# First batch's values in 1 KB pieces, key sums by one-column products, and the split of a times b one step earlier

## The chip, the cores and the metric

One core of a Trainium2 chip runs the whole kernel. The metric is the device time in microseconds (us). Matrix products run on TensorE (PE, with its weight loads PEld), elementwise work on VectorE (DVE) and ScalarE (ACT), some fills and a few tensor operations on GpSimd (POOL), and transfers are issued by SyncE (SP).

## The reference, cut to what matters

Linear attention, a gated pair of products, and a mixture of four experts, all in float32:

```python
q_s = exp(q - max(q, -1));  q_s /= sum(q_s, -1) + 1e-9
k_s = exp(k - max(k, 2));   k_s /= sum(k_s, 2) + 1e-9      # over the 576 tokens
kv  = einsum('bhsd,bhse->bhde', k_s, v)
x   = einsum('bhsd,bhde->bhse', q_s, kv)                    # then (2304, 512)
a, b = x @ w1, x @ w2                                       # 512 -> 1024
h = (a * b) @ w3;  x = h @ w_out                            # back to 512
out = sum_e p[:, e] * (relu(x @ w1[e]) @ w2[e])             # 4 experts
```

q, k and v have 4 batches, 8 heads, 576 tokens and 64 values per head. The weights of the gated pair arrive as 64-bit floats and are turned into float32 on the chip.

## The kernel before, in words

The work is written as one Python program, and a scheduler then lays down, for each engine, the order in which its instructions run; each engine takes its own list strictly in order and waits on semaphores. SP's list is one queue of transfers that has eight completion semaphores in rotation, so that a transfer also waits for the one eight places ahead of it.

Heads are taken in pairs, in the order `PAIRS`. For a pair of batch `b`, `load_k` and `load_v` (lines 185 to 205) fetch keys and values: 128 partitions hold four tokens each (512 tokens), and 64 partitions hold a tail of one token each (`KX`, the last 64). The tile of values has 65 columns per token; column 65 is filled with ones by POOL (line 197). A token's 64 values are therefore followed by a gap in the tile, and line 200 writes them in pieces of 256 bytes, while the tail is fetched by line 203. `k_max` finds the keys' largest values (DVE lines 225 to 236, PE lines 232 and 238, ACT line 244), `k_exp` subtracts and exponentiates (lines 254 and 257), and `k_v` (line 269) multiplies five times per pair: the exponentiated keys are the weights of the product, the 130 columns of values and ones stream past. The column of ones so gives the keys' sums, whose reciprocals `rs` (lines 276 and 279) scale the copy into `bd` (line 283).

Queries go through `q_exp` and `q_norm` (lines 292, 307, 311, 324 to 327) in two halves per batch, are transposed by PE (line 339), copied by ACT (line 341), multiplied by `bd` (line 352, tile `xp`), and split into a high and a low part (lines 368, 369, 373). `ab_step(c, f)` (lines 110 to 112 from line 499 on) multiplies a chunk of 512 tokens by slice `f` of both weights and stores a times b in `ah`. Each product is done in three: high by high, high by low, low by high.

The weights need a conversion (`convert`): a transfer `f64` (line 436), ACT line 141, DVE lines 145, 148, 152 and 156, and a split into `wg` (ACT line 104, DVE line 105). `unit` multiplies w3 by w_out into `W`. `h_step` splits `ah` into the two parts `h` (lines 104 and 105), which `y_step` multiplies by `W`. In the loop over `steps` (16 steps, two chunks of eight slices) the split runs four steps ahead of the product. The experts fill the rest of the run, from some 350 us on.

The first batch's part of `k_v` and the first slices of `ab_step` are what the change touches at the start of the run; the loop over `steps` is around 200 to 300 us.

Of the kernel before, what the change touches and what calls it, by code (L numbers as in the profile page):

```python
# [33 lines left out]


PAIRS = [0, 2, 1, 3]
FILL_T, FILL_B, FILL_V = (5, 3, 3, 12), (0, 3, 3, 0), (0, 0, 0, 0)
K_SLOT = [[0, 0, 0, 0], [6, 7, 8, 9], [30, 32, 34, 36], [46, 47, 48, 50]]
Q_SLOT = [[2, 2], [6, 8], [30, 34], [46, 48]]
# [17 lines left out]
def linear_attention_moe_kernel(ctx: ExitStack, tc, q, k, v, w1, w2, w3, wo, dp, e1, e2, out):  # L57
# [35 lines left out]
    def bank(pool, name):  # L93
        return pool.tile([P, 512], F32, tag="b", name=name)
# [17 lines left out]
        return nc.tensor.matmul(out=ps, lhsT=w_lo, rhs=r_hi, start=False, stop=last, **kw)  # L112

    ones = const.tile([P, 256], BF16, name="ones")
    busy = {}

    def keep_busy(n, i=None):
# [66 lines left out]
    def load_k(b, hp):  # L184
# [7 lines left out]
        ))  # L192
        kraw[b, hp] = t

    def load_v(b, hp):
        t = ap_.tile([P, 2, KR + 1, D + 1], F32, tag="vt", name="vt", bufs=4)
        nc.gpsimd.memset(t[..., D:D + 1], 1.0)
        src = v[b, 2 * hp:2 * hp + 2]
        for h in range(2):
            hold("pace" if b > 2 else ("in", b), nc.sync.dma_start(  # L200
                out=t[:, h, 0:KR, 0:D], in_=src[h, 0:KR * P].rearrange("(p r) d -> p r d", p=P)
            ))
        hold("pace" if b > 2 else ("in", b), nc.sync.dma_start(
            out=t[0:KX, :, KR, 0:D], in_=src[:, KR * P:S].rearrange("h p d -> p h d")
        ))
        vt[b, hp] = t
# [55 lines left out]
    def k_v(b, hp):  # L262
        ek, vv = ekt.pop((b, hp)), vt.pop((b, hp))
        bd = ap_.tile([P, P], F32, tag="bd", name="bd", bufs=2)
        nc.gpsimd.memset(bd, 0.0)
        ps = bank(ps_w if b == 0 else ps_a, "kv")
        for r in range(KR + 1):
            p = P if r < KR else KX
            i = nc.tensor.matmul(  # L269
                out=ps[:, 0:2 * D + 2], lhsT=ek[0:p, r].rearrange("p h d -> p (h d)"),  # L270
                rhs=vv[0:p, :, r, :], start=r == 0, stop=r == KR,
            )
        if b == 0:
            keep_busy(FILL_V[PAIRS.index(hp)], i)
        rs = ap_.tile([P, 1], F32, tag="rs", name="rs", bufs=2)
        nc.vector.tensor_scalar(
            out=rs, in0=ps[:, D:D + 1], scalar1=1e-9, scalar2=None, op0=ALU.add
        )
        nc.vector.reciprocal(out=rs, in_=rs)
        for h in range(2):  # L280
            p = slice(D * h, D * h + D)
            o = (D + 1) * h
            nc.scalar.activation(  # L283
                out=bd[p, D * h:D * h + D], in_=ps[p, o:o + D], func=ACTF.Copy, scale=rs[p]
            )
        kvb[b, hp] = bd
# [224 lines left out]
    def h_step(c, f):  # L511
        n = chunks[c][1]
        h = gran("h")
        split(h[:, 0, 0:n], h[:, 1, 0:n], prods[c, f // 2][:, f % 2, 0:n])
        if f % 2:
            del prods[c, f // 2]
        hg[c, f] = h
# [219 lines left out]

    keep_busy(14)
    make_identity(nc, ident)
    nc.scalar.activation(out=nident, in_=ident, func=ACTF.Copy, scale=-1.0)  # L740
    for i in range(4):
        load_k(0, PAIRS[i])
# [31 lines left out]
    for f in range(NF):  # L774
        convert(17 + f // 2)
        slot(W1 + f, (unit, 8 + f))
        if f % 2:
            h_step(*steps[f // 2])
    finish_lo(*prev.pop(0))
    wog.clear()  # L780
    conv.close()
# [9 lines left out]
    for i, (c, f) in enumerate(steps):  # L791
        if c == 1 and f >= NF - 2:
            load_w12(2, f - NF + 2)
        if i + 4 < len(steps):
            h_step(*steps[i + 4])
        slot(Y0 + i, (y_step, c, f))
        if i > 2:
            cook_some(2)
        if f == NF - 1:
            y_out(c)  # L800
# [298 lines left out]
```

## Time and profile before

| | us |
|---|---|
| median of 3 runs | 1159.44 |
| lowest, highest | 1158.41, 1159.78 |
| profiled execution, its own time | 1159.13 |
| span of the profiled execution | 1157.3 |
| PE busy | 1129.5 (98%) |
| DVE busy | 868.3 (75%) |
| ACT busy | 535.4 (46%) |
| POOL busy | 43.5 (4%) |

The span is what the trace covers; the profiled execution's own time lies 1.83 us above it. PE is busy nearly throughout, and where it isn't lies in the first tenth of the run. A matmul's end is modelled, so a busy PE can still be a PE that could go faster. Instructions on PE come as pairs, a weight load and the product; a float32 product without a split takes two such pairs, so that five products of line 269 are ten records.

### The profile page before, as it was taken

How to read it: one execution, taken by the hardware profiler on the slowest of the kernel's cores; microseconds unless marked ns; L12 is line 12 of the kernel's file. 1: busy time of each engine (PE TensorE's matmuls, PEld its weight loads, DVE VectorE, ACT ScalarE, POOL GpSimd, SP SyncE). 2: the span in 40 equal slices, each digit the busy share in tenths (PEclk: the TensorE clock that was granted, in tenths of full speed). 3: DMA queues.
4: the chain of work that ended last, by engine and by line, in shares of the span. 5: the costliest groups of instructions: out<-in, count | busy, mean ns of one | idle time of the engine just before them, and what ended most of it. 6: DMA issues, size and time to landing. Idle time of an engine off the chain costs nothing.

```text
span 1157.3 us, 18802 instructions
## 1 busy us (share of the span) xinstructions
PE 1129.5 (98%) x7091; PEld 1049.2 (91%) x7091; DVE 868.3 (75%) x1429; ACT 535.4 (46%) x982; POOL 43.5 (4%) x70
## 2 busy tenths in 40 slices
PE   7798999999999999999999999999999999999997
PEld 5566888788888889999999999999999999999997
DVE  7998766685558444999999987777779877777777
ACT  4775445454445325655545544334335344443441
POOL 0012100112010000000000000000000000000000
PEclk9999999999999999999999999999999999999999
DMA  9998850789899976877877888777777797777773
GB/s 236 272 351 301 322 196 1 200 288 404 311 315 369 346 290 232 294 287 281 295 271 287 280 310 304 252 247 252 247 254 258 240 308 252 253 250 251 250 253 110
DMA packets 127418, 310.12 MB, mean 268 GB/s; under 512 B 31968, under 2 KB 52960, under 8 KB 127328
## 3 DMA queue, kind: packets, MB, share of 16 engines
q1 hardware_dynamic: 126848, 308.14, 77.5%
q8 instruction: 56, 0.92, 0.3%
q10 hardware_dynamic: 480, 0.79, 0.2%
q14 instruction: 34, 0.28, 0.1%
HBM read 232.33 MB, written 76.55 MB: 267 GB/s over the span
## 4 chain that ended last, share of the span: by engine, by line
PE 87%; DVE 6%; DMA 4%; SPq 2%; issue 1%; ACT 1%; DVEq 0%; ACTq 0%
PE hp L913 30%; PE op L987 27%; PE ab L110 5%; PE ab L112 5%; PE ab L111 5%; PE y L110 3%; PE y L112 3%; PE y L111 3%; PE W L110 1%; DVE acc L971 1%; PE W L111 1%; PE W L112 1%; DMA qr<-in_q_dram 1%; PE kv L269 1%; PE xp L352 1%; DMA kr<-in_k_dram 1%
## 5 line engine op out<-in xcount | busy, mean ns | idle before, releaser
L987 PE MATMUL op<-eg,h 128*128 128x256 f32 x3024 | 379.9, 280 | 0.1
L913 PE MATMUL hp<-t,eg 128*128 128x384 f32 x2016 | 376.6, 336 | 0.9 <-DVE acc L971 0.9
L987 PEld LDWEIGHTS op<-eg,h 128*128 128x128 f32 x3024 | 373.4, 188 | 0.6 <-DVE acc L971 0.3
L913 PEld LDWEIGHTS hp<-t,eg 128*128 128x128 f32 x2016 | 344.6, 188 | 2.5 <-DVE acc L971 1.9
L971 DVE SCALAR_TENSOR_TENSOR acc<-op,prob,acc 128x256 f32<-128x256 f32 (+1 forms) x396 | 198.0, 530 | 43.1 <-PE op L987 43.1
L104 ACT ACTIVATE h<-blk 128x768 fp32r<-128x768 f32 x168 | 138.0, 843 | 142.7 <-DVE blk L614 108.9
L105 DVE TENSOR_TENSOR h<-blk,h 128x768 fp32r<-128x768 f32 x168 | 157.5, 954 | 24.4 <-ACT h L104 24.3
L896 ACT ACTIVATE blk<-hp 128x384 f32<-128x384 f32 x192 | 90.6, 489 | 142.2 <-PE hp L913 140.4
L900 DVE TENSOR_TENSOR blk<-hp,blk 128x384 f32<-128x384 f32 x144 | 79.6, 558 | 67.7 <-PE hp L913 67.2
L112 PE MATMUL ab<-x,wg 128*128 128x512 f32 (+1 forms) x320 | 119.8, 375 | 2.9 <-DVE wg L105 2.8
L110 PE MATMUL ab<-x,wg 128*128 128x512 f32 (+1 forms) x320 | 120.9, 379 | 0.9 <-ACT bd L283 0.5
L111 PE MATMUL ab<-x,wg 128*128 128x512 f32 (+1 forms) x320 | 118.7, 371 | 0.2 <-ACT x L373 0.2
L902 ACT ACTIVATE blk<-blk 128x768 f32<-128x768 f32 x72 | 60.6, 845 | 72.7 <-DVE blk L900 71.0
L614 DVE TENSOR_TENSOR blk<-blk 128x768 f32<-128x768 f32 x96 | 91.6, 954 | 0.5
L112 PEld LDWEIGHTS ab<-x,wg 128*128 128x128 f32 x320 | 60.3, 188 | 14.7 <-DVE wg L105 4.8
L110 PEld LDWEIGHTS ab<-x,wg 128*128 128x128 f32 x320 | 60.2, 189 | 12.3 <-ACT wg L104 1.4
L111 PEld LDWEIGHTS ab<-x,wg 128*128 128x128 f32 x320 | 60.4, 189 | 10.9 <-ACT x L373 1.2
L105 DVE TENSOR_TENSOR eo<-e2r,eo 128x512 fp32r<-128x512 f32 x56 | 39.1, 708 | 23.9 <-ACT eo L104 23.6
L508 DVE TENSOR_TENSOR ah<-ab,ah 128x512 f32<-128x512 f32 (+1 forms) x40 | 25.4, 635 | 40.9 <-PE ab L112 40.6
L111 PE MATMUL y<-h,W 128*128 128x512 f32 x128 | 50.2, 394 | 0.0
L112 PE MATMUL y<-h,W 128*128 128x512 f32 x128 | 49.9, 395 | 0.0
L110 PE MATMUL y<-h,W 128*128 128x512 f32 x128 | 46.8, 400 | 0.0
(101 smaller groups left out, 1044.3 us busy)
## 6 DMA issues: line engine op xcount, KB each, us to landing
eg<-e_t SPq DMA_DIRECT2D x96, 512.0 KB, 4.6
eg<-e_b SPq DMA_DIRECT2D x72, 512.0 KB, 5.0
eg<-e_s SPq DMA_DIRECT2D x68, 512.0 KB, 4.4
eg<-e_a SPq DMA_DIRECT2D x51, 512.0 KB, 4.6
wg<-w SPq DMA_DIRECT2D x48, 512.0 KB, 8.8
f<-in_moe_w_dram SPq DMA_DIRECT2D x32, 512.0 KB, 6.6
e_t<-eo SPq DMA_DIRECT2D x32, 512.0 KB, 7.5
e_s<-eg SPq DMA_DIRECT2D x28, 512.0 KB, 4.4
```

Source lines behind the costliest of these rows:

```text
L104: i = nc.scalar.activation(out=hi, in_=src, func=ACTF.Copy)
L105: j = eng.tensor_tensor(out=lo, in0=src, in1=hi.bitcast(F32), op=ALU.subtract)
L110: nc.tensor.matmul(out=ps, lhsT=w_hi, rhs=r_hi, start=first, stop=False, **kw)
L111: nc.tensor.matmul(out=ps, lhsT=w_hi, rhs=r_lo, start=False, stop=False, **kw)
L112: return nc.tensor.matmul(out=ps, lhsT=w_lo, rhs=r_hi, start=False, stop=last, **kw)
L614: return lambda: nc.vector.tensor_tensor(out=dst, in0=x, in1=y, op=op)
L896: nc.scalar.activation(out=block(name)[:, u], in_=src, func=func)
L900: nc.vector.tensor_tensor(out=x[:, u], in0=src, in1=x[:, u], op=ALU.add)
L902: nc.scalar.activation(out=x, in_=x, func=ACTF.Relu)
L913: nc.tensor.matmul(out=q, lhsT=w[:, sw, kt, P * u:P * u + P], rhs=t[b][:, kt, st], start=new and kt == 0 and i == 0, stop=kt == 1 and i == ...
L971: nc.vector.scalar_tensor_tensor(out=dst, in0=src, scalar=prob[:, T, e:e + 1], in1=dst, op0=ALU.mult, op1=ALU.add,)
L987: nc.tensor.matmul(out=q[:, c:c + DH], lhsT=g[:, sh, u, P * i:P * i + P], rhs=w[:, sw, u], start=new and u == 0 and j == 0, stop=u == 1 an ...
```

## The change

Three edits. First, the first batch's values are loaded without the column of ones: the tile is one flat row per partition, of which a view 64 or 65 columns wide is taken (`v_width`), and with 64 columns a partition's four tokens are one piece of 1 KB. Second, the keys' sums of the first batch then come from a product of their own: after each of the five products of a pair the same weights are multiplied by one column of ones (`one`), into a column of the bank behind the values. Third, the split of a times b runs five steps ahead of y instead of four, with one call more at the end of the loop before.

```diff
+V_WHOLE = (0,)
...
+    one = const.tile([P, 1], F32, name="one")
...
+    def v_width(b):
+        return D if b in V_WHOLE else D + 1
+
     def load_v(b, hp):
-        t = ap_.tile([P, 2, KR + 1, D + 1], F32, tag="vt", name="vt", bufs=4)
-        nc.gpsimd.memset(t[..., D:D + 1], 1.0)
+        t = ap_.tile([P, 2 * (KR + 1) * (D + 1)], F32, tag="vt", name="vt", bufs=4)
+        w = v_width(b)
+        t = t[:, 0:2 * (KR + 1) * w].rearrange("p (h r d) -> p h r d", h=2, d=w)
+        if w > D:
+            nc.gpsimd.memset(t[..., D:w], 1.0)
...
+        w = v_width(b)
+        s_at = D if w > D else 2 * D
...
             i = nc.tensor.matmul(
-                out=ps[:, 0:2 * D + 2], lhsT=ek[0:p, r].rearrange("p h d -> p (h d)"),
-                rhs=vv[0:p, :, r, :], start=r == 0, stop=r == KR,
+                out=ps[:, 0:2 * w], lhsT=ek[0:p, r].rearrange("p h d -> p (h d)"),
+                rhs=vv[0:p, :, r, :], start=r == 0, stop=r == KR, skip_group_check=w == D,
             )
+            if w == D:
+                i = nc.tensor.matmul(
+                    out=ps[:, 2 * D:2 * D + 1], lhsT=ek[0:p, r].rearrange("p h d -> p (h d)"),
+                    rhs=one[0:p], start=False, stop=r == KR, skip_group_check=True,
+                )
...
+    nc.gpsimd.memset(one, 1.0)
...
-        if f % 2:
-            h_step(*steps[f // 2])
+        if f % 2 or f == NF - 2:
+            h_step(*steps[f // 2 + f // (NF - 1)])
...
-        if i + 4 < len(steps):
-            h_step(*steps[i + 4])
+        if i + 5 < len(steps):
+            h_step(*steps[i + 5])
```

The scheduler answers with other orders on every engine. Line numbers of the changed kernel are larger (line 200 is 208, 203 is 211, 339 is 354, 327 is 342, 225 is 233 there); buffer numbers differ too.

SP's queue, right behind the queries of the first batch. `vt` is a pair's tile of values, `f64` raw weights, the part behind "waits" are semaphores (DMAHW5 is the sixth of the eight). Before:

```order
L200 DMA vt_128<-in_v_dram 128x4x64 [waits DMAHW4_49]
L200 DMA vt_128<-in_v_dram 128x4x64 [waits DMAHW5_49]
L203 DMA vt_128<-in_v_dram 64x2x64 [waits DMAHW6_49]
L436 DMA f64_133<-in_moe_w1_dram 128x4x256 [waits DMAHW7_49]
L436 DMA f64_133<-in_moe_w2_dram 128x4x256 [waits DMAHW0_49]
L200 DMA vt_136<-in_v_dram 128x4x64 [waits DMAHW1_49]
```

Now:

```order
L208 DMA vt_130<-in_v_dram 128x256 [waits DMAHW4_49]
L208 DMA vt_130<-in_v_dram 128x256 [waits DMAHW5_49]
L451 DMA f64_134<-in_moe_w1_dram 128x4x256 [waits DMAHW6_49]
L451 DMA f64_134<-in_moe_w2_dram 128x4x256 [waits DMAHW7_49]
L208 DMA vt_137<-in_v_dram 128x256 [waits DMAHW0_49]
L208 DMA vt_137<-in_v_dram 128x256 [waits DMAHW1_49]
L211 DMA vt_130<-in_v_dram 64x2x64 [waits DMAHW5_49,DMAHW2_49]
```

The tail of the first pair moved four places back and waits for the second large piece of its own tile (DMAHW5), five places ahead of it; the tails of the other three pairs stand thirteen, fifteen and sixteen places behind the first row, among the raw weights.

DVE's list around the second half of the first batch's queries (`qe_256` before, `qe_254` now). `kr` are keys; 351 and 451 before, 369 and 469 now, are the first two pairs of the second batch. Before:

```order
L152 SCALAR_TENSOR_TENSOR f32_473<-f64_313,f32_473 128x1024 [waits DMAHW5_49,DMAHW4_49,DVE_49]
L225 TENSOR_TENSOR m2_491<-kr_351 128x256 [waits DMAHW2_49]
L327 TENSOR_TENSOR qe_256<-qe_256,qs_343 128x1152 [waits DVE_49,PE_49]
L292 TENSOR_REDUCE qm_486<-qr_348 128x18 [waits DMAHW1_49,DMAHW0_49]
L156 SCALAR_TENSOR_TENSOR f32_473<-f64_313,f32_473 128x1024 [waits DVE_49]
L229 TENSOR_TENSOR mf_493<-m2_491 128x128 [waits DVE_49]
```

Now:

```order
L238 TENSOR_TENSOR mf_511<-mf_511,kr_369 64x128 [waits DMAHW3_49,DVE_49]
L291 TENSOR_SCALAR rs_323<-kv_312 128x1 [waits PE_49]
L233 TENSOR_TENSOR m2_584<-kr_469 128x256 [waits DMAHW7_49]
L158 SCALAR_TENSOR_TENSOR f32_491<-f64_331,f32_491 128x1024 [waits DVE_49]
L294 RECIPROCAL rs_323<-rs_323 128x1 [waits DVE_49]
L237 TENSOR_TENSOR mf_586<-m2_584 128x128 [waits DVE_49]
L339 TENSOR_REDUCE qs_361<-qe_254 128x18 [waits Activation_49]
L238 TENSOR_TENSOR mf_586<-mf_586,kr_469 64x128 [waits DMAHW2_49,DVE_49]
L340 TENSOR_SCALAR qs_361<-qs_361 128x18 [waits DVE_49]
L341 RECIPROCAL qs_361<-qs_361 128x18 [waits DVE_49]
L342 TENSOR_TENSOR qe_254<-qe_254,qs_361 128x1152 [waits DVE_49,PE_49]
```

The division of the queries (line 327, now 342) has moved behind the maxima of both key pairs of the second batch and behind the third weight pair's line 156; the first read of `kr_369` stands fourteen places above the last row.

PE's list at the same queries' transposes (line 339, now 354). Before:

```order
L112 MATMUL ab_512<-x0_2_410,wg_332 128x512
L111 MATMUL ab_526<-x0_2_410,wg_335 128x512
L112 MATMUL ab_526<-x0_2_410,wg_335 128x512
L369 MATMUL xp_408<-x1_2_417,nident_76 128x64 [waits Activation_49]
L339 MATMUL qt_376<-ident_75,qe_256 128x128 [waits DVE_49]
```

Now:

```order
L384 MATMUL xp_411<-x0_0_413,nident_76 128x224 [waits Activation_49]
L111 MATMUL ab_530<-x0_0_413,wg_350 128x512 [waits DVE_49,Activation_49]
L111 MATMUL ab_544<-x0_0_413,wg_353 128x512 [waits DVE_49,Activation_49]
L354 MATMUL qt_394<-ident_75,qe_254 128x128 [waits DVE_49]
L354 MATMUL qt_394<-ident_75,qe_254 128x128 x2
L354 MATMUL qt_399<-ident_75,qe_254 128x128 [waits PE_49]
L354 MATMUL qt_399<-ident_75,qe_254 128x128 x2
L112 MATMUL ab_530<-x0_0_413,wg_350 128x512 [waits Activation_49]
L113 MATMUL ab_530<-x0_0_413,wg_350 128x512
```

The transposes stood behind all twelve products of the head pairs 0 and 2 with the first slice; now they stand behind two of them.

## Rows read from the trace of the kernel before

**Rows 1.** Stages: PE, PEld, DVE, ACT, POOL busy, then clock, DMA share, GB/s
```profile
16.40:50.00 33.60, 24.92 (x120) 18.09 (x120) 28.81 (x50) 21.71 (x58) 1.28 (x8) 0.94 1.07 261
50.00:97.00 47.00, 41.93 (x198) 31.71 (x197) 46.44 (x75) 31.83 (x96) 8.41 (x9) 1.00 1.06 343
97.00:120.00 23.00, 20.65 (x96) 15.84 (x97) 17.96 (x29) 14.65 (x36) 2.58 (x4) 1.00 0.86 296
120.00:1157.00 1037.00, 1029.97 (x6627) 975.72 (x6627) 764.82 (x1254) 462.36 (x785) 30.03 (x37) 1.00 0.76 265
```

**Rows 2.** Who PE waited for: us in total, times, longest
```profile
PE qt L339 <- DVE qe L327: 2.9, 2, 1.7
PE ab L112 <- DVE wg L105: 2.8, 3, 1.2
```

**Rows 3.** Transfers of 18 to 20, 20 to 22 and 26 to 28 us, in this order
```profile
DMA packets 1684, 0.41 MB, mean 207 GB/s; under 512 B 1684, under 2 KB 1684, under 8 KB 1684
DMA packets 1281, 0.32 MB, mean 160 GB/s; under 512 B 1270, under 2 KB 1281, under 8 KB 1281
DMA packets 709, 0.71 MB, mean 354 GB/s; under 512 B 18, under 2 KB 709, under 8 KB 709
```

**Rows 4.** SP's list: start us, duration us, line, what is issued
```profile
11.84 2.87 SPq L200 DMA_DIRECT2D vt<-in_v_dram  x2
...
20.41 5.98 SPq L436 DMA_DIRECT2D f<-in_moe_w_dram  x6
```

**Rows 5.** Chain that ended last: the first key pair of the second batch
```profile
28.52 9.87 DMA kr<-in_k_dram
```

**Rows 6.** PE's list: start us, duration us, and idle before with its releaser
```profile
16.41 1.76 PE L269 MATMUL kv<-vt,ek 128*128 128x130 f32 x10
...
21.74 1.58 PE L269 MATMUL kv<-vt,ek 128*128 128x130 f32 x10 [0.36 <-ACT bd L283]
...
30.97 2.29 PE L352 MATMUL xp<-qT,bd 128*128 128x288 f32 x4 [2.24 <-ACT qT L341]
...
40.16 0.88 PE L339 MATMUL qt<-ident,qe 128*128 128x128 f32 x6 [1.71 <-DVE qe L327]
```

**Rows 7.** DVE's list: start us, duration us, and idle before with its releaser
```profile
16.72 0.27 DVE L236 TENSOR_REDUCE mt<-mt 128x1 f32<-128x128 f32 x1
18.20 0.16 DVE L276 TENSOR_SCALAR rs<-kv 128x1 f32<-128x1 f32 x1 [1.21 <-PE kv L269]
...
28.49 0.69 DVE L145 TENSOR_SCALAR f<-f 128x1024 f32<-128x1024 f32 x1 [1.10 <-ACT f L141]
...
38.41 0.43 DVE L225 TENSOR_TENSOR m<-kr 128x256 f32<-128x256 f32 x1 [1.31 <-DMA kr<-in_k_dram]
38.76 1.35 DVE L327 TENSOR_TENSOR qe<-qe,qs 128x1152 f32<-128x1152 f32 x1
40.02 1.35 DVE L292 TENSOR_REDUCE qm<-qr 128x18 f32<-128x1152 f32 x1
41.29 1.22 DVE L156 SCALAR_TENSOR_TENSOR f<-f,f 128x1024 int32<-128x1024 int32 x1
42.42 0.28 DVE L229 TENSOR_TENSOR mf<-m 128x128 f32<-128x128 f32 x1
...
43.89 0.42 DVE L225 TENSOR_TENSOR m<-kr 128x256 f32<-128x256 f32 x1
44.22 0.28 DVE L230 TENSOR_TENSOR mf<-mf,kr 64x128 f32<-64x128 f32 x1
44.42 0.28 DVE L229 TENSOR_TENSOR mf<-m 128x128 f32<-128x128 f32 x1
...
47.84 1.35 DVE L292 TENSOR_REDUCE qm<-qr 128x18 f32<-128x1152 f32 x1 [0.84 <-DMA qr<-in_q_dram]
...
54.79 1.27 DVE L105 TENSOR_TENSOR wg<-f,wg 128x512 fp32r<-128x512 f32 x2
```

**Rows 8.** Who waited for the tile h: us, times
```profile
PEld y L111: 0.4, 1
PEld y L110: 0.3, 1
```

More of the change, by code (lines that the diff above doesn't have):

```diff
@@ L276, in k_v @@
         nc.vector.tensor_scalar(
-            out=rs, in0=ps[:, D:D + 1], scalar1=1e-9, scalar2=None, op0=ALU.add
+            out=rs, in0=ps[:, s_at:s_at + 1], scalar1=1e-9, scalar2=None, op0=ALU.add
         )
@@ L281, in k_v @@
             p = slice(D * h, D * h + D)
-            o = (D + 1) * h
+            o = w * h
             nc.scalar.activation(
```

## The prediction, made before the run

> **What bounds the kernel now.** I read the stages first. From 120 us on PE is busy for 1029.97 of 1037 us, so nothing there can be won but by less work for PE; before it, PE stands idle for 8.68 us in 16.4 to 50, 5.07 in 50 to 97 and 2.35 in 97 to 120 [rows 1]. Whatever the change does to the time it does by these 16 us of idle time, by work added to PE, or in the y stage. In 50 to 97 DVE is the full engine: busy 46.44 of 47.00 us [rows 1]. The list of waits says the same: the largest sums behind the first 16 us are PE waiting for DVE, 2.9 us for the divided queries and 2.8 us for the split weights [rows 2]. So the end of the start-up is set by DVE: by the time at which its list, taken in order, has split the weights. And what makes DVE late is that it waits in its own list: 1.21 us for the first key sums, 1.10 for raw weights by way of ACT, 1.31 for the first keys of the second batch, 0.84 for queries, 4.46 us in all between 16.9 and 56.0 us [rows 7]. The keys of the 1.31 us were issued at 28.52 and took 9.87 us [rows 5], behind six transfers of raw weights that SP took from 20.41 to 26.39 to issue [rows 4]. The transfer queue is thus the second thing that counts, since its share is at or above 1 in the stages to 97 us [rows 1].
>
> **Part 1, the pieces of 1 KB.** Four pairs times two heads times 128 partitions times four pieces are 4096 packets of 256 bytes, 1.05 MB. While such packets ran alone they moved 207 GB/s, while 1 KB packets ran they moved 354 GB/s [rows 3]: 5.07 us against 2.96, so 2.1 us of the queue. More may be won, because around 20 to 22 us the queue ran at 160 GB/s only [rows 3] and one pair of value transfers took 2.87 us to issue [rows 4]; in the new order raw weights stand between the values and keep the queue filled. If those 2.87 us are won as well, the gain is 5.0 us. So the first keys of the second batch, which landed at 28.52 + 9.87 = 38.4 us, land between 36.3 and 33.4 us. I take 34, near the early end: the new order always has large transfers in flight there, and the slow stretch at 160 GB/s was one without them.
>
> Against it stands a new wait. The tail of the first pair now waits for the second large piece of the same tile, five places ahead, where the rotation asks for eight. Behind it on SP stand the values of pairs three and four and all later loads. What is in flight meanwhile, two raw weights of 512 KB and two values, 1.3 MB, lasts 3.7 us at 354 GB/s. SP stands still from about 13 us (11.84 [rows 4] and two issues) until the first values have landed, which they had when PE read them at 16.41 [rows 6]: 3.4 us at most, less than the 3.7. So I cost that wait at nothing. If the cover is gone, it costs up to 3.4 us, and this counts below among the late landings.
>
> **Part 2, the one-column products.** They add 20 products, 40 records on PE. No row shows one with one column. The nearest is the 130-column product: ten records take 1.58 to 1.76 us [rows 6], 0.16 to 0.18 us each. The other bound is nothing, if a record with the same weights rode along free. I take 0.15 us, near the upper end, since the weights are loaded again for each: 6 us more on PE.
>
> [...]
>
> These 6 us lie between 16.6 and 31 us, where PE had waits of 0.36 and 2.24 us among others anyway [rows 6]. The third copy of the first queries, which released PE at 30.97 [rows 6], is held on ACT by other work and comes at about the same time. But DVE reads the first key sum in order. PE now does four steps of pair one, a maximum, four of pair two, then the tail: 36 records at 0.15 from 16.6 us on, so until 22.0 us (PE read the first values at 16.41 [rows 6], with a filler product's rest still to run). DVE, from 16.92 on, fills the old 1.21 us wait with the queries' sum (1.27), a subtraction (1.27), a conversion step (0.60) and a key subtraction (0.80): it stands at 20.9 and then waits **1.0 us**. (A 128x1152 step is 1.27 us from start to start, and line 105 takes 0.60, two in 1.27 with their overlap; lines 145 and 148 have the same 0.69 record [rows 7].)
>
> **Part 3, the new order of DVE and PE.** From 22.0 us, four steps of 0.60, four of 1.13 (lines 152, 156), two of line 105, one of 1.27 and small ones, 9.96 us together, bring DVE to the first read of the new keys at 32.0 us. With a landing at 34 that is a wait of **2.0 us**, in place of 1.31. Before the division of the queries' second half DVE now has six more instructions: one line 156 (1.13), one line 225 (0.33), two each of lines 229 and 230 (0.20 each), 2.26 us [rows 7]. The division ends near 41.3 instead of 40.0. PE's transposes of it, which began at 40.16 [rows 6], follow at 41.3, and now with products behind them that used to run ahead of them. Those filled PE from 33.3 (30.97 + 2.29) to 38.45 us (40.16 - 1.71), 5.2 us with their waits [rows 6]; some stay ahead, so that PE is 2 to 4 us late at 50. In DVE's list the key maximum then waits for PE, and a query load once more; I put **1.5 us** on both, from the 0.84 of the old query wait and the lateness of PE.
>
> The balance on DVE at the split of the third weight pair, which ended at 56.0 [rows 7]: before 4.46 us of waits, now 1.0 + 2.0 + 1.5 = 4.5. By then DVE has done one key maximum more (0.33 + 0.20 + 0.20 = 0.73), so at equal work it is earlier by 0.73 + 4.46 - 4.5, some 0.7 us; I count 0.2 to 0.7 and take 0.2, as PE's lateness costs further small waits. PE's 2 to 4 us are covered by the 5.07 us for which it stood idle in 50 to 97, waiting for DVE; without that cover they would go straight to the end.
>
> **Part 4, the split five steps ahead.** PE waited for the tile h twice, 0.4 and 0.3 us [rows 8]. That is all it can give: 0 to 0.7, I take 0.35. One tile more is alive; a loss is not excluded, but no row of waits shows PE short of a tile there.
>
> **The sum.** 0.2 + 0.35 = 0.55 us less. On the profiled execution, 1159.13 us with 1157.3 of span and 1.83 around it, that is 1158.6; the median of the runs is 0.31 above it, so I say 1158.9. About 0.2% (2.3 us) is what a measurement can tell from no change.
>
> **The rivals.** *The queue's gain comes through.* If the keys land before 32 us, DVE waits for the key sum only, 1.0, and 0.5 for the rest: 4.46 - 1.5 = 3.0, with 0.2 and 0.35 it is 3.5 us, 1155.9. For it speaks that DVE is the engine that is full to 97 us and that 2.9 us of its waits were for transfers or their users; against it, that DVE now asks for the keys 6 us earlier than it did. *The keys come late.* DVE's division, and behind it PE's transposes and most of the first slice's products, now hang on the second batch's keys. If SP's wait for the tail eats the shorter packets and the keys land at 37.4, the wait is 5.4 instead of 2.0: 1158.9 + 3.4 = 1162.3. It decides for slower from a landing of 36.9 us on. For it speaks that the packets alone give 36.3, and that all three engines hang on one in-order list; against it, the 3.7 us in flight. That the change does not do what it says is possible only in part 4, where y mostly does not wait for h; it moves the sum by 0.35.
>
> **Chances.** The forecast, no difference that can be told, 0.41; the queue's gain, faster, 0.34; late keys, slower, 0.25. The likeliest case alone spans 1157.2 to 1161.2: half of the first rival's further 3.0 us are won, or the keys land at 36.3. The range of 8 in 10 reaches nearly to both other cases: 1155.4 to 1162.4.
>
> **What would show it.** The first read of the second batch's keys on DVE (line 233 there): landing near 34 and a wait near 2 us is right; no wait is the first rival, a wait over 5 us the second. The first key sum (line 291) should wait about 1 us, the 40 added records should have 0.14 to 0.16 us each, and PE should stand idle some 6 us until its transposes at 41 us, and less than 5.07 us in 50 to 97. The y stage should look as it did. What would make all of this wrong is a new stall behind 120 us, where I expect none, or waits of DVE in 50 to 97 that this order makes and I did not cost.

## The result, and the profile after

| | before | after |
|---|---|---|
| median of 6 runs each, us | 1159.61 | 1167.78 |
| lowest to highest, us | 1158.09 to 1161.20 | 1165.32 to 1170.43 |
| profiled execution, us (span) | 1159.13 (1157.3) | 1170.43 (1168.6) |
| mean granted clock of that execution | 0.995 | 0.984 |
| last four products of W start at, us | 214.67 | 218.84 |
| first product of the experts (hp) starts at, us | 440.13 | 447.21 |
| from there to the end of the span, us | 717.2 | 721.4 |

The change made the kernel slower: ratio 1.0068, 95% interval 1.0058 to 1.0078, some 8.2 us. I had said 1158.9 with a range of 1155.4 to 1162.4. The profiled execution of after was the slowest of its six runs, 2.65 us over their median, and had the lowest clock of them (their mean is 0.987), while that of before, with 0.995, lies above the 0.992 that the kernel before has on average. So the rows show what happened, and the sizes are taken from medians.

The stages of after, in the columns of [rows 1] (busy us of PE, PEld, DVE, ACT and POOL, then granted clock, DMA share, GB/s):

```profile
16.40:50.00 33.60, 29.29 (x123) 25.99 (x123) 25.70 (x47) 17.28 (x42) 0.87 (x6) 0.62 1.06 278
50.00:97.00 47.00, 44.35 (x209) 35.22 (x208) 43.30 (x76) 34.39 (x107) 7.64 (x9) 0.96 1.01 318
97.00:120.00 23.00, 20.53 (x91) 15.38 (x90) 17.16 (x25) 12.12 (x33) 1.50 (x5) 1.00 0.71 244
120.00:1168.00 1048.00, 1038.01 (x6654) 983.28 (x6652) 771.12 (x1259) 466.44 (x793) 34.90 (x39) 1.00 0.76 264
```

In the first stage PE is busy for 4.4 us more than in [rows 1], at a granted clock of 0.62 instead of 0.94, and DVE for 3.1 us less: PE was slow and DVE waited for it. Behind 120 us, where I had expected nothing, PE is busy for 8 us more, in part with work that came late (27 records more than before). The first part of it by shorter stretches, before and then after (same columns):

```profile
14.00:18.00 4.00, 4.00 (x23) 3.17 (x20) 2.99 (x5) 1.16 (x1) 0.00 (x0) 0.63 1.14 310
18.00:24.00 6.00, 3.71 (x24) 2.82 (x22) 5.80 (x12) 3.55 (x9) 0.35 (x3) 1.00 1.01 215
24.00:30.00 6.00, 4.08 (x23) 2.88 (x23) 4.83 (x11) 4.39 (x9) 0.11 (x1) 1.00 1.05 342
```
```profile
14.00:18.00 4.00, 4.00 (x24) 3.75 (x22) 4.00 (x5) 1.87 (x3) 0.00 (x0) 0.60 1.11 345
18.00:24.00 6.00, 5.56 (x27) 5.49 (x26) 3.49 (x8) 1.39 (x4) 0.12 (x1) 0.50 1.09 331
24.00:30.00 6.00, 5.35 (x25) 5.24 (x25) 6.00 (x11) 4.15 (x11) 0.23 (x2) 0.50 1.12 312
30.00:36.00 6.00, 6.00 (x29) 5.97 (x29) 3.52 (x7) 2.51 (x6) 0.12 (x1) 0.50 1.13 204
```

In both kernels the clock falls to the lower level (0.50), at 13.6 us before and 14.8 after, after PE has stood idle for 2.54 and 2.62 us. Before, it is back at 1.00 from 17 us on, but for 30.6 to 34 us; after, it stays at 0.50 until 38.7 us, although PE is hardly ever idle (busy for 16.91 of the 18 us from 18 to 36), and is low once more from 45.5 to 48.9 us, after a wait of 2.29 us. What PE does there, from its list (start us, duration us; a 32-bit product is two records):

```profile
13.43 0.30 PE L240 MATMUL mt<-ident,mf 128*128 128x128 f32 x1 [2.62 <-DVE mf L238]
13.56 1.60 PE L126 MATMUL busy<-ones 128*128 128x256 bf16 x12
14.96 0.77 PE L279 MATMUL kv<-vt,ek 128*128 128x128 f32 x2
15.52 0.43 PE L284 MATMUL kv<-one,ek 128*128 128x1 f32 x2
15.80 0.77 PE L279 MATMUL kv<-vt,ek 128*128 128x128 f32 x2
16.37 0.42 PE L284 MATMUL kv<-one,ek 128*128 128x1 f32 x2
16.66 0.78 PE L279 MATMUL kv<-vt,ek 128*128 128x128 f32 x2
```

From one L279 to the next it is 0.85 us, so a pair of heads takes 4.28 us, where [rows 6] has 1.58 to 1.76. DVE's waits in after, and SP's list:

```profile
23.34 0.16 DVE L291 TENSOR_SCALAR rs<-kv 128x1 f32<-128x1 f32 x1 [2.51 <-PE kv L284]
33.15 0.69 DVE L147 TENSOR_SCALAR f<-f 128x1024 f32<-128x1024 f32 x1 [0.32 <-ACT f L143]
36.35 0.42 DVE L233 TENSOR_TENSOR m<-kr 128x256 f32<-128x256 f32 x1 [2.51 <-DMA kr<-in_k_dram]
49.29 0.29 DVE L244 TENSOR_REDUCE mt<-mt 128x1 f32<-128x128 f32 x1 [2.39 <-PE mt L240]
```
```profile
10.65 1.35 SPq L208 DMA_DIRECT2D vt<-in_v_dram  x2
14.91 0.61 SPq L211 DMA_DIRECT2D vt<-in_v_dram  x1
15.56 2.02 SPq L208 DMA_DIRECT2D vt<-in_v_dram  x4
...
25.53 0.37 SPq L189 DMA_DIRECT2D kr<-in_k_dram  x1
```

They answer to [rows 7] and [rows 4]: three waits of 2.4 to 2.5 us and one of 0.32, 7.7 us in all against 4.46. Behind 120 us two things are new. PE stands still for 2.07 us before 243.73, behind a key maximum of DVE that took 0.42 us at 36.35 and 3.19 here, while POOL divided and subtracted (PE's row, then DVE's rows, then POOL's):

```profile
243.73 1.30 PE L367 MATMUL xp<-qT,bd 128*128 128x288 f32 x2 [2.07 <-DVE rs L291]
```
```profile
239.48 3.19 DVE L233 TENSOR_TENSOR m<-kr 128x256 f32<-128x256 f32 x1
...
243.23 0.36 DVE L106 TENSOR_TENSOR x<-xp,x 128x192 fp32r<-128x192 f32 x1 [0.40 <-ACT x L105]
243.50 0.15 DVE L291 TENSOR_SCALAR rs<-kv 128x1 f32<-128x1 f32 x1
```
```profile
238.19 2.11 POOL L342 TENSOR_TENSOR qe<-qe,qs 128x1152 f32<-128x1152 f32 x1
240.27 2.11 POOL L322 TENSOR_TENSOR qr<-qr,qm 128x1152 f32<-128x1152 f32 x1
```

The 3.19 us end at 242.67, POOL's second row at 242.38; what made the maximum take 3.19 us instead of 0.42 no run shows. The profile names the row of 243.50, the first step towards the reciprocal, as what PE waited for; by the semaphores of the built program it was the subtraction of 243.23, which frees the bank that this product writes, and which stands behind the maximum in DVE's list. In the kernel before, the maximum in that place took 2.28 us, but PE had products of y in between and waited for nothing:

```profile
237.94 2.28 DVE L225 TENSOR_TENSOR m<-kr 128x256 f32<-128x256 f32 x1
```

The second new thing is that the costliest group of products, which nothing of the change touches, takes 3.2 us more (group by form: busy us, mean ns), before and after:

```profile
L987 PE MATMUL op<-eg,h 128*128 128x256 f32 x3024 | 379.9, 280 | 0.1
```
```profile
L1003 PE MATMUL op<-eg,h 128*128 128x256 f32 x3024 | 383.1, 281 | 1.4 <-DMA eg<-e_b 1.4
```

### The profile page after: what moved, and what is told of

It reads as the page before. It is cut to its first block, busy times and chain, and to the rows that moved or that the text cites. A ratio compares the mean times of both kernels' runs of the same rounds, so it can differ in the third digit from the quotient of the medians.

```text
span 1168.6 us, 18872 instructions
## 1 busy us (share of the span) xinstructions
PE 1142.3 (98%) x7131; PEld 1067.0 (91%) x7131; DVE 867.8 (74%) x1429; ACT 535.2 (46%) x982; POOL 45.9 (4%) x67
## 4 chain that ended last, share of the span: by engine, by line
PE 88%; DVE 5%; DMA 4%; ACT 1%; SPq 1%; issue 1%; DVEq 0%; POOL 0%
PE hp L929 29%; PE op L1003 29%; PE ab L111 5%; PE ab L112 5%; PE ab L113 5%; PE y L111 2%; PE y L113 2%; PE y L112 2%; PE W L111 1%; PE W L113 1%; PE W L112 1%; DMA vt<-in_v_dram 1%; PE xp L367 1%; DMA f<-in_moe_w_dram 1%; PE kv L279 1%; DMA kr<-in_k_dram 1%
## 5 line engine op out<-in xcount | busy, mean ns | idle before, releaser
L1003 PEld LDWEIGHTS op<-eg,h 128*128 128x128 f32 x3024 | 376.1, 188 | 1.8 <-issue 1.7
L112 PEld LDWEIGHTS ab<-x,wg 128*128 128x128 f32 x320 | 60.8, 190 | 10.3 <-ACT x L388 0.6
L112 PE MATMUL y<-h,W 128*128 128x512 f32 x128 | 50.8, 398 | 0.0
L113 PE MATMUL y<-h,W 128*128 128x512 f32 x128 | 50.0, 395 | 0.0
L111 PE MATMUL y<-h,W 128*128 128x512 f32 x128 | 48.6, 405 | 0.0
```

The source lines that it names most:

```text
L111: nc.tensor.matmul(out=ps, lhsT=w_hi, rhs=r_hi, start=first, stop=False, **kw)
L112: nc.tensor.matmul(out=ps, lhsT=w_hi, rhs=r_lo, start=False, stop=False, **kw)
L1003: nc.tensor.matmul(out=q[:, c:c + DH], lhsT=g[:, sh, u, P * i:P * i + P], rhs=w[:, sw, u], start=new and u == 0 and j == 0, stop=u == 1 an ...
```

## The experiments

The theory after the first look: the one-column products hold PE at the lower clock, and the start-up loses some 5 us by it ("clock"). Rivals: the added records cost their own time whatever the clock ("records"); the loads and SP's stand for the tail set the start-up ("transfers"); the split five steps ahead does it ("split"). "Before" is timed again beside every group of runs, at 1159.5 to 1160.0.

**The split alone (e1).** The two edits of the loops that call h_step, on the kernel before.

> The kernel before with the split of a times b five steps ahead, and nothing else of the change. In the changed kernel PE stood idle for 2.07 us at 243.73, waiting for a reciprocal of key sums, and the y stage began 2 us and ended 7 us later than before. Theory "clock" (the start-up loses some 5 us because PE runs at the lower clock while it does the one-column products, and the rest comes from the order behind 190 us): the start-up to 190 us is that of the kernel before, clock 1.00 from 35 us on; the y stage may be up to 0.7 us shorter or, if the idle 2.07 us belong to this part of the change, 2 to 3 us longer; time 1158.9 to 1162.5. Rival "split" (this part carries most of the loss): 1164 or more. If 1158.9 to 1160.3 comes out, the stall at 243 us is not this part's.

1159.76 us, ratio 1.0001 (0.9992 to 1.0009); no stall at 243 us. By itself the split neither costs nor gives anything that can be told.

**The change without the split (e2).** The same two edits undone in the changed kernel.

> The changed kernel with the split of a times b four steps ahead, as before: loads of 1 KB and one-column products alone. Theory "clock": the granted clock is 0.50 from 15 to over 35 us as in the changed kernel, the last product of W comes at 219 to 220 us (214.7 before), so at least 5 us remain: 1164.5 to 1168. Rival "split": 1160 to 1162.

1173.48 us (1.0092 to 1.0123), more than the changed kernel and outside both expectations. The clock was low from 14.8 to 18.2 us, from 25 to 38.7 and again from 42 to 48.9. In place of the stall at 243.73 there are two, 2.14 us at 245.45 and 1.38 at 265.42: without the split the lists behind 190 us come out in yet another order. Between 18.2 and 25 us this run also shows the one-column products at full clock:

```profile
19.90 0.47 PE L279 MATMUL kv<-vt,ek 128*128 128x128 f32 x2
20.20 0.28 PE L284 MATMUL kv<-one,ek 128*128 128x1 f32 x2
20.34 0.47 PE L279 MATMUL kv<-vt,ek 128*128 128x128 f32 x2
...
24.22 0.46 PE L279 MATMUL kv<-vt,ek 64*128 64x128 f32 x2 [2.31 <-DMA vt<-in_v_dram]
```

From one L279 to the next 0.44 us, against 0.85 in the changed kernel: the same four records, half the time. That is 0.11 us for each record at the upper level and 0.21 at the lower. The clock rose here while such products were running, and fell again after the wait of 2.31 us, so they do not hold it down every time. The 2.31 us are the tail of values, which PE reaches before it has landed when it is quick.

**Wide products of ones (e3).** `rhs=one[0:p].to_broadcast([p, P])`, into 128 columns.

> The changed kernel, but each one-column product reads the column of ones 128 times, so it has 128 columns; instructions, loads and order stay. Theory "clock": with twice the columns per weight load the clock comes back to 1.00 within some 4 us, as it did in the kernel before (0.50 from 13.5 to 17 us); at full clock a record of 128 or 130 columns took 0.155 us there, so a pair takes 20 x 0.155 = 3.1 us instead of the 4.28 at the lower clock, though it does more work. The first sums come 1 to 2 us earlier, the first products with raw weights 3 to 5 us earlier; time 1162 to 1166. Rival "records" (40 more records cost their own time, whatever the clock): longer products, 1168 to 1170. Rival "transfers" (loads and SP's stand set the start-up): 1167.8 as before.

1168.33 us (1.0066 to 1.0090): a miss in time for "clock", and in the range of "records". But the clock did come back as "clock" said, at 17.3 us (it fell once more from 24.2 to 27.6), and the four records took 0.44 us though two of them now had 128 columns, so the width cost nothing, and a pair at full clock took 2.2 us and not the 3.1 of the expectation. The time did not fall with it. PE now waited 2.65 us for a tail at 24.08 (0.44 at 23.75 in the changed kernel), DVE read the new keys at 35.59 after a wait of 3.19 (36.35 and 2.51), and the stall of 2.07 us stood at 242.46. So the gain of the clock seems to have gone into waits for transfers: the rival "transfers" holds the next place.

**The records alone (e4).** Beside the 130-column products of the kernel before, with its own loads:

```
+            if b == 0:
+                i = nc.tensor.matmul(out=ps[:, 2 * D + 2:2 * D + 3], lhsT=ek[...], rhs=one[0:p], start=False, ...)
```

> The kernel before, loads with a column of ones and pieces of 256 bytes, and beside its 130-column products the 20 one-column products of the change, written to a spare column that nobody reads. Theory "clock": the clock stays at 0.50 far beyond the 17 us of the kernel before, to over 30 us, a pair takes 4.3 us, and 4 to 6 us are lost in the start-up: 1163 to 1166. Rival "transfers": 1159 to 1161, as nothing of the loads is changed. Rival "records" without the clock: clock back at 17 us, a pair 20 x 0.155 = 3.1 us, 6 us more on PE in a stretch where it had 8.7 us of idle time: 1160 to 1162.

1166.32 us (1.0044 to 1.0069), just above what "clock" said, and far from "transfers" and "records". The clock was 0.50 from 11.7 to 39 us, a pair took 4.3 us, and from 13.4 us on PE was not idle there:

```profile
18.00:24.00 6.00, 6.00 (x28) 5.97 (x29) 3.77 (x11) 2.13 (x6) 0.11 (x1) 0.50 1.12 245
24.00:30.00 6.00, 6.00 (x29) 5.94 (x28) 3.88 (x6) 3.85 (x9) 0.23 (x2) 0.50 1.04 340
```

**The loads without the products (e5).** The reciprocal taken of column 0, the products of L284 left out.

> The changed kernel without the one-column products: the reciprocal is taken of the first column of the keys-times-values product, so the sums of the keys of the first batch are left out. Loads of 1 KB, the wait for the tail and the split five steps ahead stay. Theory "clock" (products of one column hold PE at the lower clock, and they alone make the start-up late): the clock is back at 1.00 by 20 us, the last product of W comes at 211 to 215 us (before 214.7, changed 219.6), and since the reciprocals of the third batch here stand in DVE's list where they stood before, there is no stall of 2 us at 243: 1156 to 1160. Rival "transfers" (the tail, which SP holds back until 14.9 us and which PE waited for by 2.65 and 2.31 us at 24 us in the runs with 128 ones and without the split): PE waits 2 us or more for a tail at 21 to 24 us, keys late, 1161 to 1164.

1162.11 us (1.0007 to 1.0028), in the range of "transfers" and with its sign: PE waited 3.69 us for a tail until 24.10. The clock was back at 17.2 us, fell again at 24, behind that wait, and was 1.00 from 34.2 us on, so it can stay low for 10 us without any one-column product. The experts began 0.4 us later than in the kernel before, but then took 720.0 us instead of 717.2. Those 2.8 us are no matter of the start-up, and became the next question (below).

**The tails by themselves (e6).** Two transfers `t[0:KX, h, KR, 0:D]` for each tail of the first batch.

> The changed kernel with the tail of each pair of values of the first batch loaded by two transfers, one for each head, so that no tail waits for a large piece of its own tile; each tail now stands behind its own pieces on SP. One-column products stay. The order of DVE's reciprocals at 240 us is that of the kernel before in this build, so the stall there should be gone. Theory "clock": SP's stand from 12.0 to 14.9 us gets shorter, but PE still does its one-column products at the lower clock up to over 30 us: W's last product at 217 to 220, and less the 2 to 3 us of the stall: 1163 to 1166. Rival "transfers": the start-up becomes that of the kernel before or better, 1157 to 1160.

1170.73 us (1.0078 to 1.0112): worse, against both. PE no longer waited for a tail at 24 us, but the eight tails now stood among the pieces on SP, the first new keys were issued at 29.55 instead of 25.53, and DVE read them at 40.23 after a wait of 4.66 us. With the tails where the change puts them, the keys had thus gone out earlier. As in e2 the clock came back (at 17.2 us) while one-column products were running, and fell at 24, after a wait of 1.44 us:

```profile
18.00:24.00 6.00, 4.56 (x39) 4.43 (x38) 5.38 (x14) 3.05 (x9) 0.27 (x2) 1.00 0.56 146
```

**Fillers (e7).** `keep_busy(2, i)` behind every one-column product.

> The changed kernel with two filler products of 256 columns behind every one-column product (40 more products on PE, whose results nobody reads). At full clock a filler took 0.11 us, so PE has 4.3 us more to do. Theory "clock": the clock returns to 1.00 within 5 us and a pair takes 20 records x 0.11 + 10 x 0.11 = 3.3 us instead of 4.28; W's last product at 216 to 219 instead of 219.6, and as the reciprocals at 240 us stand where they stood before, no stall there: 1161 to 1165. Rival "records": 4.3 us more work, 1169 to 1172.

1162.16 us (1.0016 to 1.0038): 5.6 us less than the changed kernel, with 40 products more on PE. "Records" falls. The clock by stretches (as above) was not high throughout; it came back at 17.5 us, fell again behind a wait for a tail, and, with fillers between the products all the while and against the 5 us expected, rose at 34.5 us only, where the changed kernel has 38.7:

```profile
18.00:24.00 6.00, 4.23 (x39) 3.81 (x37) 5.38 (x11) 3.00 (x8) 0.11 (x1) 1.00 1.08 332
24.00:30.00 6.00, 5.14 (x28) 4.91 (x29) 2.98 (x6) 1.98 (x4) 0.11 (x1) 0.52 1.10 309
30.00:36.00 6.00, 6.00 (x34) 4.90 (x33) 3.96 (x7) 2.88 (x6) 0.11 (x1) 0.62 1.02 207
```

W's last four products started at 215.28, against 218.84 (the 219.6 of the expectations is the last of the four). In this kernel the lists at 240 us are in the order of the kernel before, and the stall is gone, so not all of the 5.6 us is the clock's.

**The stall (e8).** The key maximum of the fourth batch ordered behind that reciprocal.

> The changed kernel with one more order: the first key maximum of the fourth batch stands behind the reciprocal of the third pair of the third batch on DVE, as it does in the kernel before; in the changed kernel it stood ahead of it, took up to 3.19 us, and PE waited 2.07 us at 243.73 for that reciprocal. Theory: the start-up is that of the changed kernel (W's last product at 219 to 220), the stall and the dip of the clock behind it (0.91 in 240 to 260) go: 2 to 3 us less, 1164.5 to 1166. Rival (the stall costs nothing at the end, since PE catches up): 1167 to 1168.

1170.04 us (1.0075 to 1.0105), outside both expectations and inconclusive: 1.73 us of the stall remained at 242.97, and 1.21 at 239.67 came on top. I had taken the profile's word for the reciprocal, and a wrong one at that: the one that I put first belongs to the third pair of heads, the one in the row to the fourth. What PE waited for was the bank, and that was still freed behind a maximum. So what the stall costs by itself was not measured. The traces bound it: from the start of W's last four products to the first hp it is 228.2 to 229.8 us in the five kernels with one or two such waits of PE (changed, e3, e8, e9, e13), 233.4 in e2, and 223.8 to 225.5 in all others. That is some 3 to 5 us, the lower clock behind the stall (0.64 from 244 to 248 us in the changed kernel) and whatever else the order changes there included.

**Places in memory.** Every run with the new tile `one` had op at 381.9 to 383.4 us, every run without it 379.9 to 380.0. The tile stands in front of many others. So I asked whether the others' places count.

> The changed kernel with the new tile of ones 64 bytes wide in each partition instead of 4 (one column of it is used); every instruction and its order stay. The tile stands in front of nearly all others, so that in the changed kernel they lie 4 bytes further on. In every run with that tile the products op<-eg,h took 281 ns, in the kernel before and with the split alone 280 (busy 383.1 against 379.9 us for 3024 of them), and those of y 398 to 405 against 394 to 400. Theory "place" (the 4 bytes make each product that reads those tiles about 1 ns or more longer): op 280 ns again, the stage of experts from the first hp to the end 717 to 718 us instead of 721.4, time 1163.5 to 1166 (changed 1167.8; the start-up's low clock moves this by some 2 us). Rival (the order of the last stage makes it): 1167 to 1169.

> The kernel before with a tile of 4 bytes in each partition that is filled once and never used; the order of every engine is that of the kernel before. Theory "place": op 281 ns, the stage of experts 3 us longer, time 1162 to 1164. Rival: 1159.3 to 1160.

> The run without sums (the sums of the first batch's keys are left out, as there), with the tile of ones 64 bytes wide. That run took 1162.1, 2.6 us more than the kernel before, though its stage of experts began 0.4 us later only. Theory "place": 1158.5 to 1159.8, so the loads of 1 KB with the split gain about nothing. Rival: 1162 again, and the loads cost 2.6 us.

> The changed kernel with two fillers behind every one-column product and the tile of ones 64 bytes wide. With fillers alone it took 1162.2 and its stage of experts began 0.8 us earlier than in the kernel before. Theory "place" and "clock" together: 1158 to 1160, all of the loss accounted for. Rival to "place": 1162.

The edits are `one = const.tile([P, 16], F32)[:, 0:1]` in e9, e11 and e12, and an unused `const.tile([P, 1], F32)` in the kernel before in e10. e10 gave 1161.81 (1.0004 to 1.0023) with op at 383.0, just below the time that "place" expected. The runs with 64 bytes gave the opposite of it: 1170.16 (1.0077 to 1.0103), 1166.59 (1.0041 to 1.0079) and 1165.86 us (1.0039 to 1.0063), op at 387.1, 385.9 and 385.9. So places count, but 64 bytes are no way back. In e13, e14 and e15 I made the filler's operand 4 bytes shorter instead, 254 columns, to take the shift out, and in e16 I gave the kernel before the 64 bytes.

> The changed kernel with the filler's operand 4 bytes shorter (254 columns instead of 256), so that with the new tile of 4 bytes every later tile lies where it lies in the kernel before; the order of every engine is that of the changed kernel. Theory "place": the 3024 products op<-eg,h are busy for 379.5 to 380.5 us (383.1 in the changed kernel), time 3 us less than the changed kernel at the same clock in the start-up: 1163.5 to 1166. Rival "order": op 383 us and 1167 to 1170.

> The run with two fillers behind every one-column product, with all later tiles at the places of the kernel before (filler operand of 254 columns). Theory "place" and "clock": op 380 us instead of 382.0, time 1158.5 to 1160.5 instead of 1162.2, so that start-up and places together account for the whole loss. Rival: 1162 again.

> The run without the sums of the first batch's keys, with all later tiles at the places of the kernel before. It gives the loads of 1 KB and the split alone. Theory "place": 1158 to 1160.5 instead of 1162.1. Rival: 1162.

> The kernel before with an unused tile of 64 bytes in each partition in front of the later tiles. Theory "place": op busy for 385.5 to 387.5 us, as in the runs of the changed kernel with 64 bytes, 6 to 7 us more than before: 1165 to 1167. Rival (the 64 bytes cost only together with the new order): 1159.5 to 1163.

e16 came as expected: 1166.98 us (1.0046 to 1.0073), 7.2 us more for an unused tile, with every list in the order of the kernel before:

```profile
L989 PE MATMUL op<-eg,h 128*128 128x256 f32 x3024 | 387.1, 282 | 0.0
```

The other three changed nothing: 1167.49 (1.0051 to 1.0082), 1162.27 (1.0009 to 1.0032) and 1160.68 us (0.9998 to 1.0015), op at 383.0, 382.0 and 381.9. The reason lies in the program, not on the chip: in the built programs the tile of 4 bytes takes 32 in each partition, and the filler's operand of 508 bytes as many as that of 512. There the first tile `h` lies at byte 19008 of its partition in the kernel before and in e17, at 19040 in the changed kernel, e10 and e13 alike, at 19072 in e9, and at 18976 in e18. So these three had the same places as the runs that they were to differ from, and are repeats of them. The last two runs took out 32 bytes, by a filler of 240 columns.

> The run with two fillers behind every one-column product, with the filler's operand 32 bytes shorter (240 columns), so that every later tile really lies where it lies in the kernel before; the order of every engine is that of the run with fillers. Theory "place": op busy for 378.5 to 380.5 us instead of 382.0, from the first hp to the end of the span 717 to 718.5 us instead of 720.8, time 1158.3 to 1160.3 instead of 1162.2. Rival "order": op 382 and 1162.

> The kernel before with the filler's operand 32 bytes shorter (240 columns), so that every later tile lies 32 bytes nearer to the start; the order of every engine is that of the kernel before. If op grows by the distance alone (0, 32, 64 bytes: 380, 383, 387 us), 376 to 378 us and 1156 to 1157.5. If the places of the kernel before are the best ones, op at 381 us or more and 1160 to 1163.

```profile
L1004 PE MATMUL op<-eg,h 128*128 128x256 f32 x3024 | 378.8, 280 | 0.2
```
```profile
L987 PE MATMUL op<-eg,h 128*128 128x256 f32 x3024 | 380.4, 281 | 0.1
```

e17, the first of these rows, took 1159.63 us (0.9994 to 1.0012): the change with its fillers and with all later tiles at their old places is as fast as the kernel before, 2.5 us faster than e7 with the same lists (2.9 when each is set against the kernel before timed beside it). e18, the second, took 1159.69 (0.9991 to 1.0008), between its two expectations, so the kernel before does not gain by going 32 bytes the other way. From the first hp to the end of the span all runs fall into three groups: 716.9 to 718.1 us for no shift or 32 bytes less (before, e1, e17, e18), 719.4 to 721.4 for 32 bytes more (twelve runs), 723.9 to 724.4 for 64 (four runs).

**The account.** Six runs of the changed kernel, which differ in nothing but chance, give a price for the clock: at a mean granted clock of 0.984 they took 1170.43 and 1169.15 us, at 0.991 1165.32, on a line of 0.68 us for each 0.001 (0.6 to 0.8 in e4, e7, e8, e13 and e14 as well, anywhere from -0.3 to 1.4 in the others, of 4 to 12 runs each). It is no rule for every kernel: the 101 runs of the kernel before that were timed beside the experiments lie on a line of 0.24. The kernel before has 0.992 on average. With that, with 2.5 us for 32 bytes (e7 less e17) and 7.2 for 64 (e16), and with the stalls of PE between 230 and 270 us from each profile, estimates for the runs against the kernel before:

| run | mean clock | clock | place | stalls | sum | measured |
|---|---|---|---|---|---|---|
| changed kernel | 0.9868 | 3.5 | 2.5 | 2.1 | 8.1 | 8.2 |
| e13 | 0.9868 | 3.5 | 2.5 | 2.1 | 8.1 | 7.7 |
| e4 records alone | 0.9865 | 3.7 | 2.5 | 0 | 6.2 | 6.4 |
| e8 | 0.9848 | 4.9 | 2.5 | 2.9 | 10.3 | 10.5 |
| e7 fillers | 0.9930 | -0.7 | 2.5 | 0 | 1.8 | 2.6 |
| e5, e15 no sums | 0.991 | 0.6 | 2.5 | 0 | 3.1 | 2.6, 0.9 |
| e9 | 0.9878 | 2.9 | 7.2 | 2.1 | 12.2 | 10.1 |
| e2 without split | 0.9854 | 4.5 | 2.5 | 3.5 | 10.5 | 13.5 |
| e6 tails | 0.9850 | 4.8 | 2.5 | 0 | 7.3 | 11.2 |
| e3 wide ones | 0.9916 | 0.3 | 2.5 | 2.1 | 4.9 | 8.4 |

The sum explains the changed kernel and six of the other nine within 2.2 us; for e11, e12, e14, e10 and e17, which are not in the table, it gives 8.7, 6.2, 1.3, 2.6 and -0.5 against 6.6, 5.8, 2.5, 1.8 and -0.3. In e2, e3 and e6 some 3 to 4 us are left; there the profiles show longer waits for tails and keys and other orders (in e2 between 220 and 450 us, in e6 before 224), but I have not separated them. The stall's 2.1 us is the idle time in the profile, the lower clock behind it counts under the clock, and no run shows the two by themselves.

Two comparisons do not need the table. e4 and e10 are the kernel before with the same new tile in the same place, and differ by the 20 one-column products: 6.4 and 1.8 us over the kernel before, so these products cost 4.6 us. And over all runs of a kernel the mean clock is 0.985 to 0.988 in the seven with bare one-column products (changed, e2, e4, e6, e8, e9, e13) and 0.990 to 0.994 in those without them, with 128 columns or with fillers. So the products do lower the clock, in the mean of the runs. Why it rose among them in e2 and e6 and not in the other five stays open.

## Why the prediction was wrong, point by point

- **What bounds the kernel.** Right that behind 120 us only PE's work counts. Wrong that nothing there could change: 2.5 us came from longer products (place) and 2.1 from a stall that a new order made. I named "a new stall behind 120 us" as what would make the prediction wrong, and gave it no chance. The place of the tiles I did not think of.
- **Part 1, the pieces.** The keys were issued 3 us earlier (25.53 against [rows 5] 28.52), landed at 36.3 instead of my 34, and DVE waited 2.51 instead of 2.0: the landing is at the late end of the bounds, because the transfer took 10.80 us instead of 9.87. That the wait came out near 2.0 is luck: DVE asked for the keys at 33.84 instead of 32.0, being late itself, and at 32.0 it would have waited 4.3. Loads and split together, less 2.5 us for the place, come to +0.1 and -1.6 (e5, e15, two builds of the same work): the gain of 0.55 that I had in the sum lies between them and is neither shown nor excluded. The wait of the tail, costed at nothing with a cover, did hold SP from 12.0 to 14.91 us. It cost PE 0.44 us in the changed kernel, whose PE was late, and 2.3 to 3.7 us wherever PE was quick (e2, e3, e5, e7). My 3.4 us for the case without cover was the right size, though for another wait, PE's and not SP's; the cover was PE's own slowness.
- **Part 2, the one-column products: the step that failed.** I took the 0.16 to 0.18 us of a record in [rows 6] as a property of the work, said 0.15 for each new one, and put 6 us on PE. Its 1.58 us were taken at full clock. There the new products cost 0.13 us for two records (0.44 in e2, less 0.31 for the two records of a 130-column product), 2.6 us in all, less than I had said. But with them PE stayed at the lower level, where a record took twice the time: 4.28 us for a pair, 17.1 for four against some 6.4 before, with the 128-column products and the transposes among them slowed as well (two records of L279 took 0.77 us against 0.47 in e2; the six transposes at 29.81 took 1.54 us, six at 44.09, where the clock was 1.00, 0.88). The first sum came at 23.34 instead of 22.0, DVE waited 2.51 instead of 1.0. (My 36 records until 22.0 leave out the two of the maximum, 0.3 us.) I had these 6 us covered by idle time of PE, but for a wait of 1.0; the products cost 4.6 us by e4 and e10. I did not look at the column of the clock when I costed this part, though [rows 1] has 0.94 in just this stage.
- **Part 3, the order.** The division of the queries' second half started at 42.68 and ended at 44.0, not 41.3. I had put 1.5 us on the key maximum's wait for PE and a query; the former alone was 2.39. PE was about 6 us late at 56 (by then it had started 24 records of `ab` instead of 48, and it reached 47 at 62), not 2 to 4 at 50, and the idle time in 50 to 97 (5.07 before, 2.65 after) did not cover it. W's last products came 4.2 us late in the profiled execution.
- **Part 4, the split.** 0 by e1, inside 0 to 0.7. What I did not see is that it takes part in setting the order of the lists behind 190 us: with the rest of the change, leaving it out (e2) came with two other stalls.
- **The rivals.** Both spoke of the keys. The kernel became slower, the case with a chance of 0.25, but not for the reason given there: keys as late as that came in e6 only (landing at 40.2). None of the rivals had the clock or the places in it. The first one's 2.9 us of waits for transfers or their users are 3.25 by [rows 7].

## What to carry to other kernels

Before adding small products to PE, look at the granted clock of the stretch and at what the engine does between its idle gaps: a price read from a row holds for the clock of that row only (0.11 us for a record at 1.00, 0.21 at 0.50). Here 20 small products came with a mean clock of 0.987 instead of 0.992 and cost 4.6 us, where their own work at full clock was 2.6. If such products have to be, try wide ones among them (with fillers 5.6 of 8.2 us were gone, the stall among them) or make fewer. And when a change adds a tile, compare the duration of a group that it does not touch: if that has moved, the places of its tiles may have moved too. Here 32 bytes cost 1.8 to 2.9 us, more than the 0.55 that the change was to give.

## What was not expected of the hardware

- The stretch without gaps was the slow one. In e4 PE was busy for 12.00 of 12 us between 18 and 30, at 0.50; in the kernel before for 7.79 of them, at 1.00. So the busy time of the profile does not tell the granted clock here.
- At full clock a product with 1 column and one with 128 columns took the same: 0.44 us for the four records in e2 and in e3.
- The same products took longer with an operand at another place in its partition: op<-eg,h took 379.9 us for 3024 at the old places, 383.0 with 32 bytes more, 387.1 with 64 (e10, e16), in the same order of the lists, while hp<-t,eg stayed at 376.6, 376.1 and 376.8. In the built programs only some tiles move: `h`, the weights of op, does, while `eg` and `t` lie where they lay. So of the two operands of op only `h` has moved, and of those of hp none. Shifts of more than 64 bytes were not tried.
